# Adding the pooled attention output on the matrix engine in the first batch of an attention and gated feed-forward kernel

## The chip, the cores and the metric

The kernel runs on one core of a Trainium2 chip. The metric is the time of one execution on the device in microseconds (us), as the median of three runs. The engines are called by the names of the profile: PE is the matrix engine and PEld its weight loads, ACT is ScalarE, DVE is VectorE, POOL is GpSimd, and SP is the queue that issues most transfers.

## The reference

Shapes are 8 batches, 8 heads, 576 tokens and a head width of 64. Two attentions are added, and the sum goes through a gated feed-forward layer (512 to 1536 to 512):

```
q_d, k_d, v_d = mean over 4 neighbouring tokens of q, k, v      # 144 pooled tokens
out_up    = repeat(softmax(q_d k_d^T / 8) v_d, 4)               # each pooled row for 4 tokens
out_local = softmax(q k^T / 8 where |i - j| < 4) v              # a band of 7 tokens
x = (out_up + out_local), heads side by side                    # 4608 x 512
y = (relu(x w_gate) * (x w_val)) w_out
```

## The kernel before

The work is cut into 32 **pairs** of heads, four to a batch: pair p belongs to batch p // 4. A pair's steps carry names that the text uses with the pair's number behind them:

- `lq`, `lk`, `lv0` to `lv3`: loads of q, k and of four pieces of v, issued by SP. `cast`: q and k to 16 bits. `T`: transposes on PE; `ev0`, `ev1`, `pl`: their copies out of PSUM, `pl` being the pooled q and k.
- `Sl`, `Sd` (from pair 4 on together `S`): scores of the local and of the pooled attention. `mx`, `sub`, `exp`, `sm`, `rc`, `nrm`, `tr0`, `tr1`: the local softmax and its transposes. `dmx`, `nb` (tile `nmb`), `exd0` to `exd2` (tile `wd`), `rcd`, `nrd`: the pooled softmax. `W`, `evw` (tile `wT`): its transpose and the copy of that.
- `vc`: v to 16 bits (tile `vw`); `VP`, `vd` (tile `vdz`): v summed over four tokens on PE, and its copy.
- `V`: both products with v. The local outputs of 576 tokens lie in two PSUM banks, 288 columns in each; the pooled output of 144 columns lies behind them in the first bank. `od` (tile `od_sb`) copies the pooled output, times 0.25, to SBUF on ACT. `xa0`, `xa1` (tile `xT`) add it to the local outputs on DVE, each pooled column for four tokens.

The feed-forward layer works on chunks of tokens: `hg` and `hv` are the first products (tiles `wg_sb`, `wv_sb`; names like hg0_2 give the chunk's first token and the block of 128 of the 1536 columns), `rl` and `gm` the gate, `y` the second product (tile `wo_sb`). The first chunk needs batch 0. For columns 0 and 1 of that chunk the products are in two parts: the "a" part takes pairs 0 to 2, the "b" part pair 3.

Each step is an operation with a list of steps that it needs, one or more engines that may run it, a cost and a rank. A planner (`list_schedule`) walks through all of them once, when the program is built, and fixes the engine and the place of each. Tables of numbers by name shift the ranks (`RANKS`), delay transfers in the plan (`ASK`) and set the handicap of an engine that isn't a step's first choice (`bias`). On the chip each engine runs its steps in the planned order and waits at a step whose inputs aren't there. Where PE has nothing to do before FILL, the planner puts in products with zeros (line 1360) so that PE stays awake.

Pairs 0 to 3 are the **head** (`hd`): they run before any feed-forward work. Pairs 4 to 31 run between the products. In pairs from 8 on the transposes are transfers (`dT`, `dW`).

Of the kernel before, what the change touches and what calls it, by code (L numbers as in the profile page):

```python
# [21 lines left out]
class Op:  # L22
# [4 lines left out]
    def __init__(self, eng, dur, emit, deps=(), prio=0.0, need=None, key=None, free=(),  # L27
# [16 lines left out]
MARGIN = 0.0  # L44
# [57 lines left out]
        "lk8 cast8 ev8 pl8 mx8 exd0_8 exd1_8 nrm8 nrd8 lv0_8 lv1_8 lv3_8 vc8 VP8 V8 xa0_8 "  # L102
        "xa1_8 "
# [105 lines left out]
    ),  # L209
    -299: (  # L210
# [19 lines left out]
    ),  # L230
    -251: (
# [3 lines left out]
        "rc28 "  # L235
    ),
# [28 lines left out]
        "lk28 cast28 ev28 pl28 mx28 exp28 exd0_28 exd1_28 nrm28 nrd28 vc28 V28 xa0_28 "  # L265
        "xa1_28 "
# [10 lines left out]
    -191: (  # L277
        "pl11 "
# [95 lines left out]
    -103: (  # L374
        "pl21 "
    ),
# [14 lines left out]
        "exd0_0 exd0_3 msk16 pl27 "  # L391
# [53 lines left out]
        "T5 ev1_5 mx5 sub5 exp5 nb5 exd0_5 exd1_5 nrm5 nrd5 W5 evw5 VP5 V5 xa0_5 xa1_5 "  # L445
# [5 lines left out]
        "msk5 rc25 "  # L451
    ),
# [40 lines left out]
        "cast25 ev25 pl25 mx25 exp25 exd0_25 exd1_25 nrm25 nrd25 lv0_25 lv1_25 lv3_25 vc25 "  # L493
        "vs25 V25 xa0_25 xa1_25 "
# [4 lines left out]
    -33: (  # L499
        "lv2_26 "  # L500
    ),
    -32.5: (
        "lk26 ev26 pl26 exp26 exd0_26 exd1_26 nrm26 nrd26 lv0_26 vc26 vs26 V26 xa0_26 "
        "xa1_26 "
    ),
    -31: (
        "lk1 sub13 mx16 "
# [5 lines left out]
        "cast13 ev13 pl13 mx13 exp13 exd0_13 nrm13 nrd13 lv0_13 lv1_13 vc13 vs13 V13 xa0_13 "  # L513
# [33 lines left out]
        "dmx0 dmx1 dmx2 dmx3 vd4 dmx9 dmx11 dmx12 dmx14 dmx15 dmx16 dmx18 dmx19 dmx21 dmx22 "  # L547
        "dmx27 vc27 dmx29 dmx30 "
# [9 lines left out]
        "lv2_27 lv2_29 lv2_30 "  # L558
# [36 lines left out]
        "wg0 dmx4 sm30 "  # L595
# [9 lines left out]
    ),  # L605
    27.5: (
# [6 lines left out]
        "lk4 cast4 T4 ev0_4 ev1_4 mx4 sub4 exp4 nb4 nrm4 nrd4 W4 evw4 lv0_4 lv1_4 lv3_4 VP4 "  # L613
        "V4 xa0_4 "
# [5 lines left out]
        "y12_0 y12_1 y12_2 y14_0 y14_1 y14_2 "  # L620
    ),
# [25 lines left out]
        "cast6 T6 ev0_6 ev1_6 sub6 exp6 nb6 exd0_6 exd1_6 nrm6 nrd6 W6 evw6 lv0_6 lv1_6 "  # L647
        "lv3_6 VP6 V6 xa0_6 xa1_6 "
# [18 lines left out]
    ),  # L667
    60: (
# [9 lines left out]
        "lv0_2 "  # L678
    ),
# [56 lines left out]
    ),  # L736
    130.5: (
# [10 lines left out]
    ),  # L748
    147.5: (
        "rcd10 "  # L750
    ),
    150.5: (
        "nb31 "
# [35 lines left out]
        "cast31 ev31 pl31 mx31 exp31 exd0_31 exd1_31 nrm31 nrd31 vc31 vs31 V31 xa0_31 "  # L789
        "xa1_31 "  # L790
# [13 lines left out]
    219.5: (  # L804
        "pl23 "
    ),
    221: (
        "lv3_13 "
# [7 lines left out]
    230.5: (  # L816
        "sm25 "
    ),
# [4 lines left out]
        "sm31 "  # L823
# [11 lines left out]
        "tr0_8 sm16 pl19 exd0_19 exd1_19 "  # L835
# [61 lines left out]
    370.5: (  # L897
        "lk22 "
# [34 lines left out]
    ),  # L933
    443.5: (
# [8 lines left out]
    460.5: (  # L943
        "pl15 "
    ),
    467.5: (
        "pl6 "
# [3 lines left out]
    ),  # L951
    499: (
        "tr0_21 "
    ),
# [22 lines left out]
        "lv2_6 "  # L977
    ),
# [27 lines left out]
ASK = {"wv1": 34, "wo2": 62}  # L1006

# [63 lines left out]
def list_schedule(ops, bank_pools, eps):  # L1071
# [56 lines left out]
    while n_left:  # L1128
# [11 lines left out]
        for (i, e), s in starts.items():  # L1140
            if ends[i][1] == e and (best is None or s < best[0]):
                best = (s, e)
        assert best is not None, "the graph is stuck"
        t0, e = best
# [77 lines left out]
def kernel(  # L1222
# [10 lines left out]
    nc = tc.nc  # L1233
# [164 lines left out]
    def pair(p):  # L1398
# [325 lines left out]
        def emit_V(o):  # L1724
            for i in range(12):
                nc.tensor.matmul(  # L1726
                    out=bank[o.banks[i // 6]][:, 48 * (i % 6) : 48 * (i % 6) + 48],
                    lhsT=vw16[S3][:, i, :],
                    rhs=at2[S3][:, i, :].rearrange("p (a c) -> p a c", c=32)[:, :, 0:24],
                    start=True, stop=True)  # L1730
            n = 0
            for hh in range(2):
                for kc in range(2):
                    nc.tensor.matmul(  # L1734
                        out=bank[o.banks[0]][:, 288 : 288 + SD],
                        lhsT=vdz[S3][0:KR, hh, kc, :], rhs=wcols(hh, kc),
                        start=(n == 0), stop=(n == 3))
                    n += 1

        r["V"] = V = add(PE, 0.7 if hd else 0.56, emit_V,  # L1740
                         [*tr, vc, vdo, evw], prio=P + 40, need=(pool_, 2), key=("V", p),
                         name=f"V{p}", n=16, bias=0.0 if hd else MARGIN, late=LATE_V)
        xa = []
        t0 = b * S
        odc = add(ACT, 0.3, lambda o: nc.scalar.mul(  # L1745
            out=od_sb[S2], in_=bank[V.banks[0]][:, 288 : 288 + SD], mul=0.25),
            [V, b2.get("xa")], prio=P + 41, name=f"od{p}")
        for hf in range(2):
# [164 lines left out]
    for o in ops:  # L1913
        o.prio += SHIFT.get(o.name, 0.0)
        o.after = ASK.get(o.name, o.after)
    order = list_schedule(ops, {"F": [0, 1, 2, 3], "A": [4, 5, 6, 7]},
# [42 lines left out]
```

## Time and profile before

| | us |
|---|---|
| median of 3 runs | 364.04 (364.04 to 365.33) |
| the profiled execution | 365.24 |
| its span, first to last instruction | 363.5 |
| PE busy in the span | 352.8 (97%) |
| DVE, ACT, POOL busy | 248.4, 206.9, 201.4 |
| first feed-forward product starts | 32.60 |

The busy time of PE counts the products with zeros as well. The engines beside PE are busy for 55 to 68% of the span. The granted clock of PE is 1.00 in the whole span. What each stretch of the span is bound by is read from the stretch, not from the shares of the whole.

### The profile page before, as it was taken

Reading aid. Unit: us, or ns where it says so; the run is one execution under the profiler, and the core shown is the slowest. Engines: PE = TensorE matmul, PEld = TensorE weight load, DVE = VectorE, ACT = ScalarE, POOL = GpSimd, SP = SyncE. Lnnn points to the kernel's source line nnn. Section 1 sums busy time; section 2 is a strip of 40 time slices with the busy share of each in tenths; the row PEclk is TensorE's granted clock in tenths of the full one; section 3 lists DMA queues with packets and bytes.
Section 4 is the critical chain, followed back from the end, with each engine's and each line's share of the span. In section 5 each row is a group of like instructions: output and inputs, shape, how many; then the busy total and the mean of one; then the engine's idle time right before and its main releaser. Section 6 shows DMA issues by size and latency. Waiting matters only on the chain.

```text
span 363.5 us, 10504 instructions
## 1 busy us (share of the span) xinstructions
PE 352.8 (97%) x4241; PEld 182.2 (50%) x4241; DVE 248.4 (68%) x477; ACT 206.9 (57%) x484; POOL 201.4 (55%) x237
## 2 busy tenths in 40 slices
PE   8888999999999999999999999999989999999996
PEld 3555656445545454445444455444544454445554
DVE  4666988618987898969895986888969853322210
ACT  2477796537774757664476485768558523233222
POOL 7798574933387788683987369567785310000000
PEclk9999999999999999999999999999999999999999
DMA  7999999879999999999999999999993121011012
GB/s 189 192 276 246 192 206 301 127 181 171 272 207 214 208 276 184 271 216 253 191 220 232 172 290 165 246 239 223 200 231 81 23 85 53 0 60 59 0 70 106
DMA packets 122067, 64.80 MB, mean 178 GB/s; under 512 B 100386, under 2 KB 106402, under 8 KB 122018
## 3 DMA queue, kind: packets, MB, share of 16 engines
q1 hardware_dynamic: 116194, 59.41, 76.2%
q0 software_dynamic: 5824, 4.72, 8.6%
q8 instruction: 33, 0.54, 0.6%
q14 instruction: 16, 0.13, 0.1%
HBM read 47.59 MB, written 9.44 MB: 157 GB/s over the span
## 4 chain that ended last, share of the span: by engine, by line
PE 85%; DMA 4%; POOL 3%; SPq 2%; issue 2%; DVE 1%; ACT 1%; POOLq 0%; ACTq 0%; DVEq 0%
PE bank L1793 50%; PE bank L1859 23%; PE bank L1518 4%; DMA vw<-in_v_dram 3%; PE bank L1726 2%; PE bank L1734 2%; PE bank L1537 2%; DMA gT<-in_q_dram 1%; POOL vw L1330 1%; SPq L1675 1%; PE bank L1635 1%; PE bank L1690 1%; POOL wd L1626 1%; PE bank L1838 1%; PE bank L1456 1%
## 5 line engine op out<-in xcount | busy, mean ns | idle before, releaser
L1814 DVE TENSOR_TENSOR gT<-r,bank 128x512 f16<-128x512 f16 (+1 forms) x112 | 74.7, 667 | 65.0 <-PE bank L1793 60.6
L1793 PE MATMUL bank<-xT,wv_sb 128*128 128x512 f16 (+2 forms) x528 | 112.2, 341 | 0.9 <-ACT r L1807 0.9
L1793 PE MATMUL bank<-xT,wg_sb 128*128 128x512 f16 (+2 forms) x528 | 112.2, 341 | 0.0
L1807 ACT ACTIVATE r<-bank 128x512 f16<-128x512 f32 (+1 forms) x112 | 65.3, 584 | 65.0 <-PE bank L1793 58.1
L1859 PE MATMUL bank<-wo_sb,gT 128*128 128x512 f16 x420 | 96.6, 379 | 0.0
L1793 PEld LDWEIGHTS <-wg_sb 128*128 128x128 f16 x528 | 44.2, 98 | 46.5 <-issue 0.6
L1793 PEld LDWEIGHTS <-wv_sb 128*128 128x128 f16 x528 | 44.2, 98 | 46.0 <-issue 1.8
L1859 PEld LDWEIGHTS <-gT 128*128 128x128 f16 x420 | 39.8, 98 | 45.3 <-issue 0.4
L1868 ACT COPY y_sb<-bank 128x512 f32<-128x512 f32 x35 | 20.6, 587 | 48.7 <-PE bank L1859 48.6
L1330 POOL CAST vw<-vw 128x1536 f16<-128x1536 f32 x27 | 39.5, 1463 | 3.6 <-DMA vw<-in_v_dram 2.3
L1506 DVE TENSOR_REDUCE qkd<-qkT 128x288 f16<-128x1152 f16 x28 | 37.5, 1341 | 3.6 <-ACT qkT L1329 3.3
L1581 POOL TENSOR_TENSOR s_sb<-s_sb,mx 128x384 f32<-128x384 f32 x28 | 23.3, 833 | 27.8 <-DVE mx L1578 27.2
L1600 ACT ACTIVATE wd<-bank,nmb 128x144 f16<-128x144 f32 x96 | 35.8, 383 | 4.3 <-POOL nmb L1590 3.3
L1616 DVE STREAM_TRANSPOSE at<-e 64x384 f16<-64x384 f16 x64 | 36.4, 569 | 1.7 <-POOL e L1610 1.0
L1610 POOL TENSOR_TENSOR e<-e,rs 128x384 f16<-128x384 f16 x32 | 26.8, 841 | 16.6 <-DVE rs L1608 12.6
L1626 POOL TENSOR_TENSOR wd<-wd,rsd 128x432 f16<-128x432 f16 x32 | 29.1, 910 | 9.9 <-DVE rsd L1622 9.7
L1754 DVE TENSOR_TENSOR xT<-bank,od_sb 128x288 f16<-128x288 f32 (+2 forms) x68 | 26.8, 431 | 10.2 <-ACT od_sb L1745 10.1
L1329 ACT COPY qkT<-tq 128x1152 f16<-128x1152 f16 x23 | 27.8, 1211 | 2.9 <-DMA tq<-c 2.8
L1712 POOL TENSOR_TENSOR vs<-v 104x512 f32<-104x512 f32 x20 | 25.4, 1269 | 3.1 <-DMA v<-in_v_dram 2.8
L1587 DVE TENSOR_REDUCE nmx<-bank 128x3 f32<-128x432 f32 x32 | 19.0, 593 | 3.6 <-PE bank L1537 3.6
L1330 POOL CAST c<-qk 128x1152 f16<-128x1152 f32 x16 | 18.2, 1149 | 5.2 <-issue 2.8
L1717 POOL TENSOR_TENSOR vdz<-vs 104x256 f16<-104x256 f32 x20 | 14.6, 728 | 10.7 <-PE bank L1734 10.1
(66 smaller groups left out, 345.4 us busy)
## 6 DMA issues: line engine op xcount, KB each, us to landing
vw<-in_v_dram SPq DMA_DIRECT2D x126, 96.0 KB, 4.5
out_dram<-y_sb SPq DMA_DIRECT2D x16, 512.0 KB, 4.1
qk<-in_q_dram SPq DMA_DIRECT2D x14, 576.0 KB, 7.0
qk<-in_k_dram SPq DMA_DIRECT2D x14, 576.0 KB, 6.8
v<-in_v_dram SPq DMA_DIRECT2D x10, 640.0 KB, 7.8
wv_sb<-in_moe_w_val_dram POOLq DMA_DIRECT2D x4, 384.0 KB, 10.4
wg_sb<-in_moe_w_gate_dram POOLq DMA_DIRECT2D x4, 384.0 KB, 10.0
wo_sb<-in_moe_w_out_dram POOLq DMA_DIRECT2D x4, 384.0 KB, 8.1
```

Source lines behind the costliest of these rows:

```text
L1329: return lambda o: nc.scalar.copy(out=dst, in_=src(o))
L1330: return lambda o: engine[eng].tensor_copy(out=dst, in_=src(o))
L1506: nc.vector.tensor_reduce(out=qkd[S3].rearrange("p (x t) -> p x t", x=2), in_=qk_sums, axis=AX.X, op=ALU.add)
L1600: exd.append(add(ACT, 0.37, lambda o, i=i: nc.scalar.activation(out=_sap(wd_, 0, 128, 256 * i + K0, kd_cols), in_=_sap(dview()[:, i, :], 0 ...
L1610: r["nrm"] = nrm = add_any(either(lambda o, e: e.tensor_tensor(out=e_, in0=e_, in1=bc12(rs[S3]), op=ALU.mult), (POOL, 0.84), (DVE, 0.5)), ...
L1616: tr.append(add(DVE, 0.575, lambda o, lo=lo: nc.vector.transpose(out=at2[S3][lo : lo + 64, :, lo // 2 : lo // 2 + 32], in_=e_[lo : lo + 64 ...
L1626: r["nrd"] = nrd = add_any(either(lambda o, e: e.tensor_tensor(out=_sap(wd_, 0, 128, K0, w3), in0=_sap(wd_, 0, 128, K0, w3), in1=_sap(rsd[ ...
L1754: nc.vector.tensor_tensor(out=xT[:, kk, (c1 + lo) % XR : (c1 + lo) % XR + hi - lo].rearrange("p (t f) -> p t f", f=4), in0=bank[V.banks[hf ...
L1793: nc.tensor.matmul(out=bank[(h or o).banks[0]][:, n * x : n * x + n], lhsT=w_sb[:, kk, bass.ts(jj, 128)], rhs=xT[:, kk, x_col(t0) : x_col( ...
L1807: rl = add(ACT, 0.17 + 0.00083 * n * m, lambda o: nc.scalar.activation(out=rt[:, 0 : n * m], in_=bank[f1.banks[0]][:, 0 : n * m], func=AF. ...
L1814: gm = add(DVE, 0.15 + 0.00104 * n * m, lambda o: nc.vector.tensor_tensor(out=gT[:, js[0] : js[0] + m, pos : pos + n], in0=rt[:, 0 : n * m ...
L1859: nc.tensor.matmul(out=bank[parts[0].banks[0]], lhsT=gT[:, jj, col : col + 128], rhs=wo_sb[:, jj, :], start=(jj == 0), stop=(jj == NJJ - 1))
```

## The change

In pairs 0 to 3 the pooled output is no longer a separate product. After the twelve local products, eight more with 288 columns each add the pooled output into the same two banks; their moving operand reads each of 72 pooled columns four times. So `od` and the additions on DVE go, and `xa0`, `xa1` of these pairs become plain copies from PSUM that ACT or DVE may run. The factor 0.25 moves into the matrix that sums v, for all pairs that use it (0 to 11). Core of the diff:

```
-            sums[x, i, 12 * i + 6 * par[x] + (r[x] - 3) // 4] = 1.0
+            sums[x, i, 12 * i + 6 * par[x] + (r[x] - 3) // 4] = 0.25
...
-                    start=True, stop=True)
+                    start=not hd or i % 6 == 0, stop=not hd)
+            if hd:
+                for hf in range(2):
+                    for n in range(4):
+                        nc.tensor.matmul(
+                            out=bank[o.banks[hf]][:, 0:288], lhsT=vdz[S3][0:KR, n // 2, n % 2, :],
+                            rhs=_sap(wT[S3], 0, KR, n * SD + 72 * hf, [[1, 72], [0, 4]]),
+                            start=False, stop=(n == 3))
+                return
...
-        r["V"] = V = add(PE, 0.7 if hd else 0.56, emit_V,
+        r["V"] = V = add(PE, 1.35 if hd else 0.56, emit_V,
...
+        if not hd:
+            odc = add(ACT, 0.3, ... mul=1.0 if p < VPOOL else 0.25 ...)
+        for hf in range(2 * hd):
+            xa.append(add_any(copies(
+                xT[:, kk, x_col(t0 + 288 * hf) : x_col(t0 + 288 * hf) + 288],
+                lambda o, hf=hf: bank[V.banks[hf]][:, 0:288], (ACT, 0.41), (DVE, 0.45)),
+                [V], prio=P + 42 + hf, free=[("V", p)], name=f"xa{hf}_{p}"))
-        for hf in range(2):
+        for hf in range(0 if hd else 2):
...
-            if ends[i][1] == e and (best is None or s < best[0]):
+            if ends[i][1] == e and (best is None or (s, e != POOL) < best[:2]):
```

The last line lets POOL go first where two engines could start a step at the same planned time. The tables change as well: the shifts of 38 names in `RANKS` are other ones, a second table of shifts (`MORE`, 332 names), a second one of delays (`ASKED`) and a table of handicaps (`STAY`) are new. A line of each:

```
+    -250.0: (
+        "rc20 lv3_24 "
+    ),
...
+ASKED = {"wg2": 29.5, "wg3": 42.0, "wo1": 58.5}
...
+        "sub5 ev8 ev9 ev11 ev12 ev13 ev14 ev15 ev16 ev17 ev18 ev19 ev20 ev21 ev23 ev24 ev25 "
```

So the order changes on every engine. Three places are shown. The first is the queue of SP, from the load of pair 2's q (`gT` takes q and k of the head, `vw_64` to `vw_67` are the v buffers of pairs 0 to 3). Before:

```order
L1430 DMA gT<-in_q_dram 48x2x768
L1675 DMA vw_65<-in_v_dram 32x12x64 x3
L1675 DMA vw_64<-in_v_dram 32x12x64
L1669 DMA vw_64<-in_v_dram 29x64
L1675 DMA vw_64<-in_v_dram 32x11x64
L1675 DMA vw_64<-in_v_dram 32x12x64
L1430 DMA gT<-in_q_dram 48x2x768
L1675 DMA vw_66<-in_v_dram 32x12x64
L1430 DMA gT<-in_k_dram 48x2x768
```

The same place after the change:

```order
L1783 DMA gT<-in_q_dram 48x2x768 x2
L1783 DMA gT<-in_k_dram 48x2x768
L2028 DMA vw_64<-in_v_dram 32x12x64 x2
L2028 DMA vw_66<-in_v_dram 32x12x64
L2028 DMA vw_65<-in_v_dram 32x12x64
L2022 DMA vw_64<-in_v_dram 29x64
L2028 DMA vw_64<-in_v_dram 32x11x64
L2028 DMA vw_65<-in_v_dram 32x12x64 x2
L2028 DMA vw_66<-in_v_dram 32x12x64
```

Pair 3's q and k stand ahead of the v pieces now, and the last two pieces of pair 1's v (`vw_65`) stand behind those of pair 0.

The second place is POOL in the head (`wo_sb<-gT` are the casts of q and k, `nmb` the step nb, `e` the step nrm, `wd` the step nrd, `vw` the step vc). Before:

```order
L1330 CAST wo_sb<-gT 96x2x12x64 x3
L1380 DMA wv_sb<-in_moe_w_val_dram 128x4x384
L1380 DMA wg_sb<-in_moe_w_gate_dram 128x4x384
L1590 ISA
L1590 TENSOR_SCALAR nmb_129<-nmx_126 128x3
L1590 TENSOR_SCALAR nmb_130<-nmx_127 128x3
L1610 TENSOR_TENSOR e_92<-e_92,rs_123 128x384
L1610 TENSOR_TENSOR e_93<-e_93,rs_124 128x384
L1330 CAST vw_84<-vw_64 128x1536
L1330 CAST vw_85<-vw_65 128x1536
L1330 CAST wo_sb<-gT 96x2x12x64
L1590 TENSOR_SCALAR nmb_131<-nmx_128 128x3
```

After:

```order
L1683 CAST wo_sb<-gT 96x2x12x64 x3
L1733 DMA wv_sb<-in_moe_w_val_dram 128x4x384
L1733 DMA wg_sb<-in_moe_w_gate_dram 128x4x384
L1683 CAST wo_sb<-gT 96x2x12x64
L1943 ISA
L1943 TENSOR_SCALAR nmb_129<-nmx_126 128x3
L1963 TENSOR_TENSOR e_92<-e_92,rs_123 128x384
L1963 TENSOR_TENSOR e_93<-e_93,rs_124 128x384
L1943 TENSOR_SCALAR nmb_130<-nmx_127 128x3
L1683 CAST vw_85<-vw_65 128x1536
L1943 TENSOR_SCALAR nmb_131<-nmx_128 128x3
L1979 TENSOR_TENSOR wd_99<-wd_99,rsd_135 128x6x3x24
```

The cast of pair 3's q and k moves ahead of the first nb, and vc of pair 0 leaves POOL (it is on ACT now, as is vc of pair 2).

The third place is ACT, up to the last copies that the first feed-forward product needs (`xT` is what that product reads). Before, where the product needs what DVE adds behind the third od:

```order
L1584 ACTIVATE e_92<-s_sb_91 128x384
L1745 ACTIVATE od_sb_112<-bank_145 128x144
L1600 ACTIVATE wd_99,smd_132<-bank_144,nmb_129 128x2x3x24
L1745 ACTIVATE od_sb_113<-bank_138 128x144
L1600 ACTIVATE wd_99,smd_132<-bank_144,nmb_129 128x2x3x24 x2
L1329 CAST vdz_98<-bank_140 96x2x2x64
L1745 ACTIVATE od_sb_112<-bank_139 128x144
```

After, where the last two rows are the copies of pair 2:

```order
L1682 CAST xT<-bank_142 128x288
L1953 ACTIVATE wd_99,smd_132<-bank_143,nmb_129 128x2x3x24 x2
L1682 CAST xT<-bank_145 128x288
L1682 CAST vw_86<-vw_66 128x1536
L1682 CAST xT<-bank_138 128x288
L1682 CAST xT<-bank_141 128x288
L1682 CAST vdz_98<-bank_140 96x2x2x64
L1682 COPY wT_102<-bank_144 96x6x2x48
L1682 CAST xT<-bank_138 128x288
L1682 CAST xT<-bank_139 128x288
```

All eight copies of the head stand on ACT, and vc of pair 2 stands among them.

On PE the head now runs to V2, then VP3, the first product's first part (hg0_0a) and V3. Behind the head PE has the same steps as before in nearly the same order; towards the end some steps of pairs 28 to 31 stand earlier among the products.

More of the change, by code (lines that the diff above doesn't have):

```diff
@@ L230 @@
     ),
+    -253: (
+        "V1 "
+    ),
     -251: (
@@ L667 @@
     ),
+    59: (
+        "pl11 "
+    ),
     60: (
@@ L736 @@
     ),
+    130: (
+        "T4 "
+    ),
     130.5: (
@@ L803 @@
     ),
-    219.5: (
-        "pl23 "
+    214: (
+        "pl25 "
+    ),
+    217.5: (
+        "pl26 "
     ),
     221: (
-        "lv3_13 "
+        "pl13 lv3_13 "
     ),
@@ L951 @@
     ),
+    480.5: (
+        "sm25 "
+    ),
     499: (
         "tr0_21 "
+    ),
+    500: (
+        "pl19 "
     ),
@@ L1008 @@
+STAY = {name: by for by, names in STAY.items() for name in names.split()}
 EV = (1.2, 1.2, 0.68)
@@ L1915 @@
         o.after = ASK.get(o.name, o.after)
+        o.bias = STAY.get(o.name, o.bias)
+    for o in ops:
+        o.prio += MORE.get(o.name, 0.0)
+        o.after = ASKED.get(o.name, o.after)
+        o.bias = STAY.get(o.name, o.bias)
     order = list_schedule(ops, {"F": [0, 1, 2, 3], "A": [4, 5, 6, 7]},
```

419 lines of the change are left out of this document (370 added, 49 removed), and 5 rows, old and new, of the table MORE.

## The prediction

> **What bounds the kernel now.** I read the windows first: the busy time of each engine in stretches of the span. The columns are the stretch, its length, and the busy time with the number of instructions of PE, PEld, DVE, ACT and POOL.
>
> ```profile
> 0.00:33.00 33.00, 27.61 (x485) 15.74 (x486) 21.23 (x49) 17.11 (x50) 26.83 (x37) 1.00 1.06 229
> ...
> 41.00:100.00 59.00, 58.59 (x940) 31.77 (x938) 43.75 (x80) 39.12 (x94) 33.23 (x38) 1.00 1.02 209
> 100.00:200.00 100.00, 100.00 (x1202) 50.05 (x1194) 82.81 (x160) 62.33 (x155) 77.43 (x89) 1.00 1.08 224
> 200.00:300.00 100.00, 98.85 (x1184) 49.49 (x1183) 80.39 (x158) 61.96 (x144) 59.19 (x70) 1.00 0.89 178
> ```
>
> From 41 us to 300 us PE is busy for 257.4 of 259 us. What it does there is fixed by the reference and is the same after the change, so a microsecond lost or won ahead of 41 us reaches the end whole, and behind it there are only 1.6 us to win. The head is another matter: there PE waits for the other engines (zeros fill part of it), and its length is set by them. The chain of waits shows by which (start, length, engine and line):
>
> ```profile
> 18.17 2.73 POOL vw L1330 x2
> ...
> 30.50 0.92 POOL wd L1626
> ...
> 32.77 1.29 PE bank L1793 x6
> ...
> 42.85 0.45 PE bank L1518 x48
> ```
>
> Two vc casts on POOL, then POOL's normalising steps, and with them the first feed-forward products (the last row is for a price below). So the head now hangs on POOL. The timeline of PE shows where the products begin and what is lost before they run without holes:
>
> ```profile
> 32.60 0.81 PE L1793 MATMUL bank<-xT,wg_sb 128*128 128x512 f16 x3
> ...
> 34.33 0.68 PE L1456 MATMUL bank<-ident_sb,c 128*128 128x128 f16 x9
> 34.84 0.81 PE L1793 MATMUL bank<-xT,wg_sb 128*128 128x512 f16 x3
> ...
> 36.69 0.67 PE L1456 MATMUL bank<-ident_sb,c 128*128 128x128 f16 x9
> 38.02 0.52 PE L1518 MATMUL bank<-qkT 64*32 64x32 f16 x48 [0.67 <-DVE xT L1754]
> ...
> 40.10 1.02 PE L1793 MATMUL bank<-xT,wg_sb 128*128 128x512 f16 x4
> ```
>
> The start is 32.60. At 36.69 the transposes of pair 4 begin; such a set takes 34.84 - 34.33 = 0.51, so PE is free at 37.20 and waits 0.82 for the scores of pair 5 (a bank that DVE's additions of pair 3 hold). That is the one large hole between the start and 40.10.
>
> **The change, part by part.** *V of the head.* The price of the eight new products comes from the chain: the twelve local and the four pooled products of a V, and twelve feed-forward products with 512 columns in a row:
>
> ```profile
> 58.43 0.30 PE bank L1726 x12
> 58.73 0.25 PE bank L1734 x4
> ...
> 63.24 2.59 PE bank L1793 x12
> ```
>
> A product with 512 columns takes 2.59 / 12 = 0.216, so one with 288 takes 0.121 and eight take 0.97. Less the 0.25 of the four old ones, each V of the head grows by 0.72, from 0.55 to 1.27. No row has a moving operand that reads an element four times. The nearest is a step of two elements in the local scores of pairs from 8 on:
>
> ```profile
> 84.98 0.45 PE bank L1518 x48
> ...
> 85.64 0.33 PE bank L1690 x6
> ```
>
> With a step of one, in pair 4, the same 48 products took the same 0.45 (the row of 42.85 above). So a step costs nothing there, and I take full speed; the other bound is half speed (rival four).
>
> *What starts ACT.* POOL's queue has pair 3's cast ahead of the first nb. These rows of the timeline set its price (13.97 is used below):
>
> ```profile
> 13.97 1.57 SPq L1430 DMA_DIRECT2D gT<-in_k_dram  x1
> ...
> 15.12 0.76 POOL L1380 DMA_DIRECT2D wg_sb<-in_moe_w_gate_dram  x1
> ...
> 16.28 0.38 ACT L1600 ACTIVATE wd<-bank,nmb 128x144 f16<-128x144 f32 x1 [0.52 <-POOL nmb L1590]
> ```
>
> POOL is done with its second weight load at 15.88, and ACT's first pooled exponential follows 0.40 later; nb is 0.24 of that (a row below), so a hand-over costs some 0.08. With a cast of 1.46 in between, ACT starts at 17.74.
>
> *ACT's queue.* From there to the copies of pair 2, on which the first product waits, ACT has 29 steps in the new order. Their mean times in the head (all groups of ACT and of POOL between 11 and 33 us, name and shape, count, busy us and mean ns):
>
> ```profile
> L1600 ACT ACTIVATE wd<-bank,nmb 128x144 f16<-128x144 f32 x12 | 4.5, 390 | 1.5 <-POOL nmb L1590 1.5
> ...
> L1329 ACT COPY wT<-bank 96x576 f16<-96x576 f16 x4 | 2.6, 640 | 2.0 <-PE bank L1635 2.0
> ...
> L1584 ACT ACTIVATE e<-s_sb 128x384 f16<-128x384 f32 x4 | 2.1, 525 | 3.2 <-DVE s_sb L1571 3.2
> L1329 ACT CAST vdz<-bank 96x256 f16<-96x256 f32 x3 | 1.1, 363 | 0.2 <-PE bank L1690 0.2
> L1329 ACT CAST qkd<-bank 128x288 f16<-128x288 f32 x2 | 0.8, 423 | 0.0
> ```
>
> ```profile
> L1330 POOL CAST vw<-vw 128x1536 f16<-128x1536 f32 x4 | 5.8, 1462 | 0.0
> ...
> L1330 POOL CAST wo_sb<-gT 96x1536 f16<-96x1536 f32 x2 | 2.9, 1464 | 2.3 <-DMA gT<-in_q_dram 2.3
> ...
> L1590 POOL TENSOR_SCALAR nmb<-nmx 128x3 f32<-128x3 f32 x4 | 0.9, 242 | 1.0 <-DVE nmx L1587 0.9
> ```
>
> And a vc on ACT, from later pairs:
>
> ```profile
> L1329 ACT CAST vw<-vw x5: 1466/1474/1486, 53.0 to 269.8; 128x1536 f16<-128x1536 f32 x5
> ```
>
> Twelve exponentials at 0.39 are 4.68, two vc at 1.47 are 2.95, one pl at 0.42, two exp at 0.53 are 1.05, three vd at 0.36 are 1.09, three evw at 0.64 are 1.92, and six copies to `xT` at 0.42 (the shape of `qkd`) are 2.54: 14.65 in all. Without a wait ACT is through at 17.74 + 14.65 = 32.4. Two kinds of waits come on top. While PE runs V2 for 1.27, ACT has one evw of 0.64 to do, so it stands for 0.63. And it waits for another engine at sub2, W0, V0 and W3, for a hand-over each at least, 0.3 together. So the copies end at 33.4, and with PE's own hand-over of 0.1 the first product starts at 33.5: **0.9 later than 32.60**. POOL no longer sets the head; ACT does, since it took over two vc and the copies while it lost three od (and DVE lost the additions).
>
> *PE behind the start.* From 32.60 to 40.10 PE takes 7.50 now. The hole of 0.82 goes: V3 and the copies of pair 3 come before the transposes of pairs 4 and 5, and the copies are on ACT. VP3 (0.33, the row of 85.64 above) stands ahead of the start now, and V3 is 0.72 longer. That makes 0.82 + 0.33 - 0.72 = **0.4 won back**. What is late next there is the pl of pair 4, a step of DVE; it starts as soon as T4 is copied, and DVE no longer has additions ahead of it.
>
> *The v pieces.* In SP's queue pair 3's q and k pass the v pieces. The last piece of pair 1's v is SP's 22nd transfer now; before, the 22nd was issued at 13.97 (the row above). Where a load stands in this queue matters, since the weight loads of POOL start just then. Packets of the two queues (q0 is POOL's, q1 SP's) from 17 to 18.5 us, and from 20 to 22 us:
>
> ```profile
> q0 software_dynamic: 359, 0.28, 124.4%
> q1 hardware_dynamic: 19, 0.00, 1.4%
> ```
>
> ```profile
> q0 software_dynamic: 369, 0.28, 89.8%
> q1 hardware_dynamic: 359, 0.09, 34.0%
> ```
>
> And the time from issue to landing of a v piece issued at 13.33, and of the two issued from 15.59 on:
>
> ```profile
> DMA to landing us min/median/max: 4.4/4.4/4.4
> ...
> DMA to landing us min/median/max: 8.2/8.2/8.3
> ```
>
> I put the issue at 14.5, so the piece lands between 18.9 and 22.7; I take the middle, 20.8. POOL's vc of pair 1 waits for it, and behind it in POOL's queue stand nb2 and all nrd. ACT reaches the exponential that needs nb2 at 17.74 + 6 x 0.39 + 1.47 + 0.42 + 0.36 = 22.3, so vc must start by 22.3 - 0.24 - 1.46 - 0.16 = 20.4. **0.4 late**, and ACT's whole rest shifts by it.
>
> [...]
>
> *Behind 41 us* PE has the same steps, so I cost the moved ones at nothing. The cover is that their inputs are there when PE comes; rivals two and three say what it is worth.
>
> *The sum:* 0.9 - 0.4 + 0.4 = 0.9. The profiled execution took 365.24 (1.7 outside its span), which makes 366.1; it ran 1.2 above the median of 364.04, which makes **364.9** for the median.
>
> **The rivals.** *One: the v piece is starved to the end.* It lands at 22.7, 2.3 behind the point of 20.4 from which it decides: 364.5 + 2.3 = **366.8**, slower. For it: SP's queue got 19 packets in 1.5 us. Against it: that stretch fell behind a load of q and k, and here only two v pieces are in question.
>
> *Two: faster.* The piece is in time (364.5), and PE's waits behind the head go. These are the three that stand there now:
>
> ```profile
> 60.69 0.19 PE L1518 MATMUL bank<-qkT 64*32 64x32 f16 x2 [0.41 <-issue]
> ...
> 263.75 0.41 PE L1734 MATMUL bank<-wT,vdz 104*128 104x144 f16 x4 [0.30 <-DMA wT<-wd]
> ...
> 271.83 1.02 PE L1793 MATMUL bank<-xT,wv_sb 128*128 128x512 f16 x4 [0.85 <-ACT r L1807]
> ```
>
> Without their 1.56 it is 362.9, and without ACT's waits of 1.0 in the head 361.9; the middle is **362.4**. For it: the new order moves work from POOL to ACT and DVE in later pairs. Against it: the waits come from transfers and from ACT, not from POOL.
>
> *Three: PE waits more behind 200 us.* Scores and V of pairs 28 to 31 stand earlier among the products, and an engine that runs in order waits there. With two more waits of 0.85 and one of 0.30: 364.9 + 2.0 = **366.9**. For it: DVE is busy for 80 of 100 us there, so a step has little room to be earlier. Against it: only three waits in 259 us now.
>
> *Four: reading one element four times runs at half speed.* V2 and V3 lie on the path, 0.97 more each: 364.9 + 1.9 = **366.8**. The scores with step two speak against it.
>
> **How the numbers follow.** A measurement of this kernel can tell 0.5%, 1.8 us, from no change: faster is below 362.2, slower above 365.9. I give my forecast 0.42, and since its landing time alone spreads by 2 us, 0.10 of that is slower and 0.32 the same. Rival one has 0.18 (0.15 slower, 0.03 same), two 0.25 (0.12 faster, 0.13 same), three 0.10 (0.08 slower, 0.02 same), four 0.05 (0.04 slower, 0.01 same). That makes 0.12 faster, 0.51 the same, 0.37 slower. The range runs from rival two to just above rivals one, three and four, 362.3 to 367.0; about 2 in 10 lie outside.
>
> **What would show it.** Right: the first feed-forward product at 33.5 to 34, ACT without a gap between 17.7 and the copies of pair 2 except at V2, the hole of 0.82 gone, V of the head at 1.27. Wrong: a first exponential of ACT near 16.3; POOL idle before vc of pair 1 until 22 (rival one); products of 288 columns at 0.25 apart (four); waits of over 1 us on PE behind 41 us (three). A first product before 32.6 would break the reading that ACT bounds the new head.

## The result and the profile after

The changed kernel takes **368.89 us** (median of six runs, 366.61 to 374.82) against 364.35 for the kernel before. The run of 374.82, at a clock of 0.986, counts as slow and is left out of the ratio. That ratio is 1.0091, 95% interval 1.0063 to 1.0119, or 3.3 us slower; the two medians lie 4.5 apart. The forecast was 364.9 in a range of 362.3 to 367.0.

The profiled execution took 366.61, with a span of 364.8. It was the fastest of the six, and its granted clock is 1.000; the four others that count took 367.73 to 369.08 at a clock of 0.991 to 0.995. The windows after, with the columns of those before:

```profile
0.00:33.00 33.00, 27.92 (x486) 16.48 (x487) 21.60 (x47) 17.45 (x49) 24.47 (x35) 1.00 1.07 228
...
41.00:100.00 59.00, 59.00 (x893) 32.23 (x892) 46.15 (x85) 36.73 (x93) 34.62 (x39) 1.00 1.01 205
100.00:200.00 100.00, 98.87 (x1258) 49.76 (x1256) 83.74 (x162) 64.85 (x151) 69.88 (x81) 1.00 1.06 220
200.00:300.00 100.00, 99.33 (x1173) 49.42 (x1171) 85.03 (x160) 63.99 (x150) 58.92 (x70) 1.00 0.91 185
```

POOL has lost 2.4 us of work in the head, yet the head isn't shorter. PE's timeline tells a part of why (in brackets the idle time ahead of a row and what ended it; "issue" is a wait for nothing that the profile shows):

```profile
17.95 0.24 PE L1813 MATMUL bank<-ident_sb,wo_sb 96*128 96x96 f16 x2 [2.04 <-issue]
...
24.69 0.30 PE L1871 MATMUL bank<-qkT 64*32 64x32 f16 x20 [0.84 <-issue]
...
33.92 0.90 PE L2161 MATMUL bank<-xT,wg_sb 128*128 128x512 f16 x3
...
40.29 1.04 PE L2161 MATMUL bank<-xT,wg_sb 128*128 128x512 f16 x4
...
178.72 1.02 PE L2161 MATMUL bank<-xT,wv_sb 128*128 128x512 f16 x4 [0.35 <-ACT r L2175]
194.96 0.41 PE L2096 MATMUL bank<-wT,vdz 104*128 104x144 f16 x4 [0.77 <-DMA wT<-wd]
247.25 0.41 PE L2096 MATMUL bank<-wT,vdz 104*128 104x144 f16 x4 [0.65 <-DMA wT<-wd]
```

The first row is in the middle of one step: ten of the twelve transposes of pair 2's k ran, then PE stood for 2.04 us, and then came the last two. The view names no data that it waited for. The trail starts in the queue table of the page, and in that table for 15.0 to 16.6 us (queue, packets, MB, share of 16 engines):

```profile
q8 instruction: 33, 0.54, 0.6%
```

```profile
q8 instruction: 1, 0.02, 5.1%
```

PE's instructions come in 33 transfers of 16 KB, one for every 256 weight loads and products (2 x 4252 in all), so a block holds 128 products with their loads. In the 17 profiles of this document 24 waits of over 0.25 us behind 10 us are marked "issue". By a count of PE's products all 24 stand 94 or 95 of them behind a multiple of 128, and PE goes on 1.25 to 1.65 us after a block's landing. So such a wait is **a block of instructions that came late**. In the packets of that queue the block in question lands at 16.50, and PE goes on 1.45 later. Before, the same block landed at 15.14, and PE went on at 16.62 after a stop of 0.48. The rows of POOL and ACT behind the stop:

```profile
17.58 0.26 POOL L1943 TENSOR_SCALAR nmb<-nmx 128x3 f32<-128x3 f32 x1
...
21.06 1.46 POOL L1683 CAST vw<-vw 128x1536 f16<-128x1536 f32 x1 [1.46 <-DMA vw<-in_v_dram]
```

```profile
18.23 0.40 ACT L1682 CAST qkd<-bank 128x288 f16<-128x288 f32 x1 [1.87 <-PE bank L1813]
18.52 0.39 ACT L1953 ACTIVATE wd<-bank,nmb 128x144 f16<-128x144 f32 x1
```

The first nb is done at 17.84, but `pl2` stands ahead of the exponentials in ACT's queue and needs those two last transposes. PE's row at 24.69 is the next block end, 128 products on.

For an account I take three marks: the first feed-forward product, the first product of the second chunk (hg576_0; behind it PE has work nearly without holes), and PE's last product.

| profile of | first product | hg576_0 | last product | from hg576_0 to the last | clock |
|---|---|---|---|---|---|
| before | 32.60 | 77.48 | 360.15 | 282.67 | 1.000 |
| changed | 33.92 | 77.83 | 361.53 | 283.70 | 1.000 |
| changed, again | 35.05 | 78.96 | 363.35 | 284.39 | 0.995 |
| addition alone (`add_only`) | 33.03 | 77.82 | 359.67 | 281.85 | 0.999 |
| all moves and 119 pairs (`all_119`) | 33.15 | 77.05 | 364.93 | 287.88 | 1.000 |
| addition and 21 pairs (`add_21`) | 31.84 | 76.63 | 359.45 | 282.82 | 1.000 |

In the first profile 0.35 is lost up to hg576_0 and 1.03 behind it.

### The profile page after: what moved, and what is told of

Read it like the earlier page. It is cut to its first block, busy times and chain, and to the rows that moved or that the text cites. A ratio compares the mean times of both kernels' runs of the same rounds, so it can differ in the third digit from the quotient of the medians.

```text
span 364.8 us, 10513 instructions
## 1 busy us (share of the span) xinstructions
PE 354.9 (97%) x4252; PEld 184.0 (50%) x4252; DVE 254.3 (70%) x480; ACT 206.9 (57%) x484; POOL 194.3 (53%) x230
## 4 chain that ended last, share of the span: by engine, by line
PE 78%; DMA 11%; POOL 3%; ACT 3%; issue 2%; SPq 2%; DVE 1%; ACTq 0%; POOLq 0%
PE bank L2161 43%; PE bank L2227 22%; DMA wT<-wd 4%; DMA vw<-in_v_dram 3%; PE bank L1871 3%; DMA gT<-in_q_dram 3%; PE bank L2079 2%; PE bank L2096 2%; DMA tq<-c 1%; PE bank L1890 1%; ACT wd L1953 1%; PE bank L2043 1%; PE bank L1988 1%; PE bank L2206 1%; POOL vs L2065 1%
## 5 line engine op out<-in xcount | busy, mean ns | idle before, releaser
L1683 POOL CAST vw<-vw 128x1536 f16<-128x1536 f32 x23 | 33.6, 1463 | 5.7 <-DMA vw<-in_v_dram 2.9
L1979 POOL TENSOR_TENSOR wd<-wd,rsd 128x432 f16<-128x432 f16 x31 | 28.1, 908 | 11.1 <-DVE rsd L1975 9.2
L1934 POOL TENSOR_TENSOR s_sb<-s_sb,mx 128x384 f32<-128x384 f32 x27 | 22.4, 831 | 17.7 <-DVE mx L1931 17.4
L1963 POOL TENSOR_TENSOR e<-e,rs 128x384 f16<-128x384 f16 x29 | 24.0, 831 | 13.7 <-DVE rs L1961 10.5
L2122 DVE TENSOR_TENSOR xT<-bank,od_sb 128x288 f16<-128x288 f32 (+2 forms) x60 | 23.3, 427 | 8.3 <-ACT od_sb L2108 7.8
L1682 ACT COPY qkT<-tq 128x1152 f16<-128x1152 f16 x21 | 25.1, 1199 | 3.9 <-DMA tq<-c 3.9
L1683 POOL CAST c<-qk 128x1152 f16<-128x1152 f32 x15 | 17.1, 1147 | 15.2 <-DMA qk<-in_k_dram 8.2
L1871 PEld LDWEIGHTS <-qkT 64*32 64x32 f16 x1536 | 13.6, 90 | 12.9 <-issue 9.0
L1953 ACT ACTIVATION_READ_ACCUMULATOR wd<-bank,nmb 128x1 f32 x96 | 19.8, 206 | 0.0
```

Source lines behind the costliest of these rows:

```text
L1682: return lambda o: nc.scalar.copy(out=dst, in_=src(o))
L1683: return lambda o: engine[eng].tensor_copy(out=dst, in_=src(o))
L1871: nc.tensor.matmul(out=scv[32 * c : 32 * c + 32, i, :], lhsT=cols(hh, q0 + step * 24 * blk, 32), rhs=cols(hh, k0 + step * (24 * blk - 3), 32),
L1953: exd.append(add(ACT, 0.37, lambda o, i=i: nc.scalar.activation(out=_sap(wd_, 0, 128, 256 * i + K0, kd_cols), in_=_sap(dview()[:, i, :], 0 ...
L1979: r["nrd"] = nrd = add_any(either(lambda o, e: e.tensor_tensor(out=_sap(wd_, 0, 128, K0, w3), in0=_sap(wd_, 0, 128, K0, w3), in1=_sap(rsd[ ...
```

## The experiments

"Clock low" counts the runs whose mean clock was below 0.998.

| kernel | median us | ratio to before, 95% interval | clock low |
|---|---|---|---|
| before, beside the sets of runs below | 364.63 to 364.79 | | 5 of 68 |
| again | 368.23 | 1.0091 (1.0059 to 1.0123) | 6 of 10 |
| add_only | 365.27 | 1.0015 (0.9996 to 1.0035) | 0 of 12 |
| tables_only | 381.54 | 1.0433 (1.0398 to 1.0468) | 6 of 6 |
| vpiece | 367.54 | 1.0076 (1.0049 to 1.0104) | 4 of 10 |
| early_rcd | 368.83 | 1.0088 (1.0061 to 1.0116) | 5 of 6 |
| dw_ahead | 369.46 | 1.0112 (1.0080 to 1.0145) | 5 of 6 |
| three | 368.25 | 1.0074 (1.0047 to 1.0102) | 4 of 6 |
| zeros4 | 369.79 | 1.0122 (1.0076 to 1.0168) | 3 of 6 |
| after_119 | 368.25 | 1.0106 (1.0059 to 1.0153) | 2 of 6 |
| all_119 | 369.78 | 1.0135 (1.0095 to 1.0175) | 0 of 6 |
| before_stop | 364.50 | 0.9987 (0.9960 to 1.0015) | 5 of 12 |
| before_119 | 368.46 | 1.0102 (1.0061 to 1.0143) | 4 of 6 |
| before_75 | 369.19 | 1.0112 (1.0088 to 1.0137) | 5 of 6 |
| add_75 | 369.57 | 1.0124 (1.0098 to 1.0149) | 6 of 6 |
| add_21 | 363.41 | 0.9949 (0.9927 to 0.9971) | 1 of 10 |

**The changed kernel again.** 

> The changed kernel once more, unaltered, to see where its runs differ from its profiled execution (366.61 us at a granted clock of 1.000, while its other runs took 367.7 to 369.1 at 0.991 to 0.995). Theory (instructions and clock): PE stands for 2.04 us at 15.9 us because its next instructions land late, and with so little done there the clock of PE falls to a half for one stretch in most runs: median 368 to 369, mean clock 0.991 to 0.996, and in a profile with a clock below 1.000 the low stretch lies between 13 and 27 us, some 3.4 us long (0.005 x 367 = 1.8 us of lost clock). Rival (transfers): the runs differ by waits for transfers behind 41 us; then the low clock is a by-product, lies behind 41 us, and PE shows waits of over 1 us there.

Its profile is one at 0.995, and it shows where the clock was low (windows of 1 us; the third number from the right is the clock):

```profile
18.00:19.00 1.00, 0.47 (x4) 0.28 (x4) 0.09 (x1) 0.19 (x1) 1.00 (x3) 1.00 1.30 197
19.00:20.00 1.00, 1.00 (x15) 0.84 (x14) 0.48 (x1) 1.00 (x6) 0.85 (x2) 0.78 1.32 228
20.00:21.00 1.00, 1.00 (x15) 0.97 (x13) 0.80 (x2) 1.00 (x1) 0.00 (x0) 0.50 1.32 206
21.00:22.00 1.00, 1.00 (x63) 0.63 (x60) 0.53 (x1) 1.00 (x5) 0.00 (x0) 0.50 1.26 219
22.00:23.00 1.00, 1.00 (x14) 0.28 (x3) 0.64 (x2) 1.00 (x6) 0.66 (x1) 0.51 1.39 255
```

The loss is 0.22 + 0.50 + 0.50 + 0.49 = 1.71, so PE ran at half clock for 3.4 us. What stands ahead of that stretch, and behind 41 us, in PE's timeline, and POOL's vc of pair 1:

```profile
18.53 0.24 PE L1813 MATMUL bank<-ident_sb,wo_sb 96*128 96x96 f16 x2 [2.73 <-issue]
...
247.96 0.41 PE L2096 MATMUL bank<-wT,vdz 104*128 104x144 f16 x4 [1.75 <-DMA wT<-wd]
271.32 0.41 PE L2096 MATMUL bank<-wT,vdz 104*128 104x144 f16 x4 [1.12 <-DMA wT<-wd]
```

```profile
22.34 1.47 POOL L1683 CAST vw<-vw 128x1536 f16<-128x1536 f32 x1 [2.49 <-DMA vw<-in_v_dram]
```

The theory holds: the stop was longer, and the clock was low behind it, in the head. Of the rival, the waits behind 41 us came as well (V24 and V27 waited 2.87 for their transposed weights), but the clock wasn't low there. The v piece of pair 1 landed at 22.19 in place of 20.91. By the clock, the ten runs and the other five of the first set part into medians of 367.43 (five runs at 1.000) and 368.80 (nine at 0.995). Their ranges overlap, so the clock goes with 1.4 us and isn't all of it.

**The addition alone, and the tables alone.** The first has the addition with the tables and the tie-break of before; the second the new tables with the pooled product, `od` and the additions of before.

```
-RANKS = { ... }; MORE = { ... }; ASKED = { ... }; STAY = { ... }
+RANKS = { as before }; MORE, ASKED, STAY = {}, {}, {}
```

> The addition on PE alone, with the tables and the tie-break of before. Theory (instructions and clock): SP's queue in the head is that of before, so PE's instructions come as before (a stop of at most 0.6 us near 16 us), the clock stays at 1.000, and the time is that of before plus the longer V: 364.0 to 365.5. Rival (the addition itself costs): V2 and V3 lie on the path, two times 0.72 and the copies on ACT: 366 to 368. A faster kernel than before (under 363.5) would say that the tables cost what the addition won.

> The new tables and the tie-break with the pooled product, od and the additions of before. Theory (instructions and clock): SP's queue in the head is the new one, PE stands for about 2 us near 16 us and the clock falls below 1.000 in most runs: 367 to 369. Rival (the addition itself costs): 363.5 to 365, clock 1.000.

Near 16 us both theories hold. PE stands for 0.31 with the tables of before and for 2.14 with the new ones, whatever the pooled product (`add_only`, then `tables_only`):

```profile
16.37 1.89 PE L1363 MATMUL bank<-r 128*128 128x512 f16 x8 [0.31 <-issue]
```

```profile
17.93 0.24 PE L1813 MATMUL bank<-ident_sb,wo_sb 96*128 96x96 f16 x2 [2.14 <-issue]
```

The addition alone is level with the kernel before, although it shows a stop of its own, in the middle of V2:

```profile
32.24 0.41 PE L1738 MATMUL bank<-wT,vdz 96*128 96x288 f16 x2 [1.11 <-issue]
```

So **the tables cost what was lost, not the addition**: the changed kernel is `add_only` with the new tables (and the tie-break), and took 3.0 more in the same set of runs (368.23 against 365.27). By the marks above, its two profiles lose 0.01 and 1.14 against `add_only` up to hg576_0, and 1.85 and 2.54 behind it. The tables alone came out far worse than any theory had it. They shift ranks in a plan that was found with V's new length. My reading, which no run shows, is that the order falls apart without it; the longest waits stand in later pairs, where V isn't even changed:

```profile
198.61 0.52 PE L1871 MATMUL bank<-qkT 64*32 64x32 f16 x48 [2.88 <-ACT qkT L1682]
...
280.19 0.52 PE L1871 MATMUL bank<-qkT 64*32 64x32 f16 x48 [3.27 <-ACT qkT L1682]
```

It is no measure of the tables in their own plan. The next kernels leave the plan as it is and move single steps in the finished order.

**Single steps moved.** `vpiece`, `early_rcd`, and both with a third move (`three`):

```
+    ("lv0_2", "behind", "lv3_1"),                                   # vpiece
+    ("rcd24", "behind", "exd2_24"), ("nrd24", "ahead of", "vc25"),  # early_rcd
+    ("rcd27", "behind", "exd2_27"), ("nrd27", "ahead of", "vd29"),
+    ("pl2", "behind", "exd1_0"),                                    # three, with all above
```

> The changed kernel with one transfer of SP moved: the piece lv0_2 (pair 2's, which nobody needs before 29 us) goes behind lv3_1, the last piece of pair 1, which is then SP's 21st transfer in place of the 22nd. All else stands as it is. In two profiles of the changed kernel that piece landed at 20.91 and at 22.19, and V0 started at 26.44 and at 27.71: 1.28 and 1.27 apart. Theory (three losses: the v piece, the instruction stop with the clock, late wT behind 180 us): the piece lands by 20.8, POOL's vc of pair 1 starts by 21 in the profile, and the median falls by 0.3 to 1.0, to 367.3 to 368.0. Rival (the stop at 16 us alone sets the head): no difference, 368.2.

> The changed kernel with four steps of pairs 24 and 27 moved ahead: rcd behind the last exponential of its pair on DVE, nrd ahead of a vc (pair 24) and of a vd (pair 27) on POOL. The transfers dW24 and dW27, which V24 and V27 wait for (0.65 to 1.75 and 0 to 1.83 us in three profiles), can be issued 1 to 3 us earlier; the order on PE, ACT and SP stands as it is. Theory (late wT): no wait over 0.3 at V24 and V27 in the profile, and the median falls by 1.0 to 2.5, to 365.7 to 367.2. Rival (transfers are slow whatever their issue): the waits stay, 367.8 to 368.8.

> The changed kernel with the moves of the last two kernels of this name's set together (lv0_2 behind lv3_1; rcd and nrd of pairs 24 and 27 ahead) and one more: ACT's copy pl2 behind the first two pooled exponentials, so that ACT does not stand at it while PE's transposes of pair 2 wait for instructions (ACT started its exponentials at 18.52 and 19.10 in two profiles, while nb was there at 17.84 and 18.08). Theory (three losses): first pooled exponential at about 17.9, first feed-forward product by 33.5, no wait over 0.4 behind 41 us; median 364.5 to 366.3, 2 to 4 below the changed kernel. Rival (clock sets it): clock at 0.995 in half the runs and 366.5 to 368.

`vpiece`: POOL's vc of pair 1 waits for nothing; the median is 0.7 lower, as expected, but the intervals overlap. In its place the scores of pair 2 end last, which nb2 waits for by way of DVE (POOL's timeline):

```profile
19.15 1.45 POOL L1686 CAST vw<-vw 128x1536 f16<-128x1536 f32 x1
21.76 0.23 POOL L1946 TENSOR_SCALAR nmb<-nmx 128x3 f32<-128x3 f32 x1 [1.16 <-DVE nmx L1943]
```

`early_rcd`: V27's wait is gone, V24's isn't. SP's timeline shows why (POOL was done with nrd24 at 237.67):

```profile
239.87 0.61 SPq L1789 DMA_DIRECT2D qk<-in_k_dram  x1
240.57 1.96 SPq L2008 DMA_TRANSPOSE wT<-wd  x1
```

```profile
248.59 0.41 PE L2102 MATMUL bank<-wT,vdz 104*128 104x144 f16 x4 [2.07 <-DMA wT<-wd]
```

The transfer stood for 2.9 us in SP's queue behind the loads of later pairs. `three` has ACT's first exponential at 17.49, but also a stop of 2.01 and 6.8 us at half clock (3.42 lost from 17 to 25 us), and the scores of pair 2 came so late that nb2 stood 2.69; its first product is at 35.39. In this profile the moves in the head win nothing.

**The loads behind dW24 and dW27.**

```
+    ("lq28", "behind", "dW24"), ("lk28", "behind", "lq28"),         # with early_rcd's moves
+    ("lv0_30", "behind", "dW27"), ("lv1_30", "behind", "lv0_30"), ("lv3_30", "behind", "lv1_30"),
```

> The changed kernel with rcd and nrd of pairs 24 and 27 moved ahead, as in the kernel that moved these alone, and with SP's loads that stood ahead of the transfers dW24 (q and k of pair 28) and dW27 (three v pieces of pair 30) put behind them. In the kernel that moved rcd and nrd alone, nrd24 was done at 237.7 and dW24 still went out at 240.6, behind those loads, and V24 waited 2.07. Theory (SP's queue makes wT late): no wait over 0.4 at V24 and V27, median 366.0 to 367.4. Rival (the transfers are slow at that place whatever the order): the waits stay at 1 to 2 and the median at 368 or above.

V24's wait went; V27 still waited 1.41, and a new wait of 1.11 for ACT's `wd` came at 274.86. The theory holds for V24 alone, and the time did not fall: with one of 0.41 at 259.52, PE's waits behind 41 us still come to 2.9.

**Instruction blocks shifted.** Products with zeros at the start are cut into more and shorter ones, which moves every block's end to an earlier place in the program. `zeros4` and the 75-pair kernels cut 25 of them into four, the 21-pair kernels 7 into four, the 119-pair kernels 17 into eight.

```
+            for g in range(4):
+                c = slice(128 * g, 128 * g + 128)
+                nc.tensor.matmul(out=bank[i][:, c], lhsT=r1[0][:, 0:128], rhs=r1[0][:, c], ...
```

> The changed kernel with its first 25 products with zeros cut into four of 128 columns each, the same order otherwise: 75 more pairs of weight load and product stand ahead of the first scores, so the ends of PE's instruction blocks lie elsewhere in the head. Theory (instructions and clock): the stop of 2.04 us at 15.9 goes (the block that ends there now ends 75 pairs earlier, in the middle of the first scores, and was asked for while the zeros ran), ACT's first pooled exponential comes at about 17.7 in place of 18.5, the clock is 1.000 in most runs, and the median falls from 368.9 to 364.5 to 366.5; a shorter stop may appear at 13 us. Rival (queues): PE waited for data, not for instructions; the stop stays at 15.9 and the time at 368 to 369.

> The kernel before with its first 7 products with zeros cut into four of 128 columns each: 21 more pairs of weight load and product ahead of the first scores, the order otherwise that of before. PE's instruction block then ends 21 pairs earlier, at about 14.3 us in place of 16.1, while it is asked for at about the same time. Theory (instructions and clock): PE stops for 1.5 to 2.4 us at 14.3 us, the clock falls to a half for 3.4 us in some of the runs (mean 0.995), and the median rises by 0.7 to 2.5, to 365.4 to 367.2. Rival (PE in the head has time; POOL sets its length): 364.3 to 365.2 and a clock of 1.000.

> The kernel before with its first 17 products with zeros cut into eight of 64 columns (and 32 rows of output) each: 119 more pairs of weight load and product ahead of the first transposes, the order otherwise that of before. PE's instruction blocks of 128 pairs then end 119 pairs earlier in the program, where its own trace gives 6.4 to 7.6 us between the ends (at 11.99, 18.35, 25.95, 33.47 us), about as long as a block took to come. Theory (instructions): no stop of PE over 0.3 between 11 and 34 us other than for data, the clock at 1.000 in nearly all runs, and 363.0 to 364.2, below the kernel before (364.7). The runs of the kernel with 21 more pairs that kept the clock took 363.1 to 364.9, those at 0.995 took 364.9 to 367.6. Rival (POOL sets the head): 364.4 to 365.0.

> The changed kernel with the same 119 pairs more ahead of the first transposes. Theory (instructions and clock): the stop of 2.0 to 2.8 at 15.9 us goes, the clock is 1.000 in most runs, the first feed-forward product starts at 33.3 to 34.0, and the median falls by 0.8 to 2.0, to 366.3 to 367.5; the late wT behind 180 us stays. Rival (the v piece and POOL set the head, whatever the clock): first product at 33.9 to 35.0 and 367.8 to 368.5.

> The changed kernel with all of it together: 119 pairs more ahead of the first transposes, lv0_2 behind lv3_1 on SP, pl2 behind the first two pooled exponentials on ACT, and rcd, nrd and dW of pairs 24 and 27 ahead. Theory (three losses, each with its place): no stop at 16 us, clock 1.000 in most runs, first feed-forward product by 33.4, no wait over 0.4 at V24 and V27: 363.5 to 365.5, no slower than the kernel before (364.7). Rival (something else costs): over 366.5 although the three are gone.

`zeros4` and `after_119`: the stop at 16 goes, as the theory says, but PE then waits for POOL's cast of pair 3 (`after_119`, and 1.30 in `zeros4`):

```profile
18.30 0.68 PE L1817 MATMUL bank<-ident_sb,wo_sb 96*128 96x96 f16 x12 [1.29 <-POOL wo_sb L1683]
```

ACT's exponentials start at 18.45 and 18.58, no earlier than with the stop, and the time doesn't fall. `after_119` has the clock (four of six runs) and the first product (33.75) of its theory but the time of its rival; `zeros4` lies above the ranges of both. Under the stop there was a second bound.

`before_stop` splits by the clock. The stop came (first row), 1.45 in place of 0.48, and the clock was low behind it:

```profile
16.14 0.50 PE L1462 MATMUL bank<-ident_sb,wo_sb 96*128 96x96 f16 x8 [1.45 <-issue]
```

```profile
18.00:19.00 1.00, 1.00 (x4) 0.43 (x3) 0.99 (x3) 1.00 (x6) 1.00 (x2) 0.50 1.32 216
19.00:20.00 1.00, 1.00 (x4) 0.31 (x3) 0.95 (x3) 1.00 (x6) 1.00 (x2) 0.50 1.12 331
```

Its five runs at 0.995 have a median of 365.29, the seven at 1.000 one of 363.20: a low stretch goes with 2.1 within one kernel, of which the clock itself takes 1.7. None of the seven was profiled, so whether the stop was as long in them isn't shown.

`all_119` has every move and no stop at 16. All six runs kept the clock (0.999 or 1.000), the first product is at 33.15, and hg576_0 is at 77.05, earlier than in either kernel, although the next block end still stops PE for 0.94 at 24.0 us. So its head is no longer behind. Behind hg576_0, 4.2 more is lost than in the changed kernel's first profile (287.88 against 283.70). Eight waits of 0.3 to 0.9 there come to 4.9, against 1.8 in three; which of the moves brought them was not separated. One of them:

```profile
261.79 0.37 PE L1911 MATMUL bank<-qkd 64*32 64x144 f16 x12 [0.86 <-ACT od_sb L2129]
```

`before_119` missed: stops came up behind the head, where none were.

```profile
62.39 0.28 PE L1545 MATMUL bank<-qkd 64*32 64x144 f16 x5 [1.11 <-issue]
102.97 0.28 PE L1526 MATMUL bank<-qkT 64*32 64x32 f16 x17 [1.67 <-issue]
```

Yet the clock of that profile is low in the head, from 21.94 us on, where PE had waited for data alone (the longest for 0.81). `add_75` has the same from 21.79 us. The stretch just ahead of it in `before_119`, with PE busy for 1.74 of 3.41 us:

```profile
18.53:21.94 3.41, 1.74 (x71) 0.91 (x72) 3.30 (x9) 2.76 (x12) 3.41 (x4) 1.00 1.23 190
```

So a stop for instructions isn't the only thing that the clock fell behind.

**The addition with shifted blocks.**

> The kernel before with its first 25 products with zeros cut into four of 128 columns each, 75 pairs more ahead of the first scores. By its own trace the instruction blocks then end at 12.81, 19.27, 26.31 and 36.97 us, 6.5 to 10.7 apart, so at most one short stop near 13 is left in the head. Theory (instructions and clock): clock 1.000 in most runs, 363 to 364.5. Rival (a shift only moves the stops, also those behind the head, as 119 pairs did, which put 1.1 and 1.7 us of them at 62 and 103 us): 364.7 to 367.

> The addition on PE with the tables of before and 75 pairs more ahead of the first scores, as in the kernel before with 75 pairs. The stop of 1.11 inside V2 goes if the blocks end at 26.2 and 37.4 as its trace says. Theory (the addition is level by itself, and that stop hid a small gain): 0.3 to 1.2 below the addition alone (365.3), 364.0 to 365.0, and within 0.7 of the kernel before with the same shift. Rival (the addition costs, by V2 and V3 on the path): 1 or more above the kernel before with the same shift.

> The addition on PE with the tables of before and 21 pairs more. The kernel before with 21 pairs took 363.1 to 364.9 where the clock stayed and 364.9 to 367.6 where it fell. Theory: the same split by the clock here, about 363.5 to 365 at 1.000 and 1.5 to 2.5 more at 0.995, so that one stretch at half clock in the head costs 1.2 to 2.3. Rival (the clock follows the lateness and does not cause it): the runs at 0.995 are spread over the same range as those at 1.000.

With 75 pairs a block ends behind or among small products at 101 us. PE stood 2.49 (`before_75`) and 3.30 (`add_75`), and the clock was low with it (0.65 from 105 to 108 us in `add_75`):

```profile
103.73 1.02 PE L1799 MATMUL bank<-xT,wg_sb 128*128 128x512 f16 x4 [2.49 <-DVE at L1622]
```

```profile
104.00 0.40 PE L1546 MATMUL bank<-qkd 64*32 64x144 f16 x5 [3.30 <-issue]
```

The view credits the first wait to a step of DVE that was done 0.76 before PE went on. By its place, 94 products behind a multiple of 128, and by the landing 1.30 ahead, it is a block end like the others. So the shift moved the stops, as `before_75`'s rival says, and at a higher price than the 364.7 to 367 that it named. `add_75` is within 0.7 of `before_75`, as its theory says, but not at 364 to 365. With 21 pairs the addition alone is **0.5% below the kernel before**: 363.41, ratio 0.9949 (0.9927 to 0.9971).

```profile
15.88 0.50 PE L1465 MATMUL bank<-ident_sb,wo_sb 96*128 96x96 f16 x8 [1.31 <-issue]
...
31.84 0.81 PE L1817 MATMUL bank<-xT,wg_sb 128*128 128x512 f16 x3
```

At a full clock it is level with the kernel before at the same 21 pairs (362.86 to 364.55 against 363.06 to 364.90), so the gain goes with the shift, and nothing is won or lost by the addition. Its clock fell once in ten runs. That run took 364.45, inside the range of the others, so the price that was expected of a low stretch doesn't show here. Why the clock fell so much less often than in `before_stop`, with a stop of 1.31 against 1.45, is open.

## Why the prediction was wrong

*V of the head* was right. The eight products take 0.98 in the chain, 0.97 was forecast; rival four is out.

```profile
32.68 0.98 PE bank L2088 x8
```

*What starts ACT* was 0.8 too early: nb was there at 17.84, near the forecast start of 17.74, but ACT started at 18.52. The step took only POOL's nb as the start and left out `pl2`, which stands ahead of it and waited for PE. The first product still came at 33.92, in the span given as right (33.5 to 34), but that is luck. From its first exponential to the end of pair 2's copies ACT was busy for 13.0 us and stood for 2.9, where 14.65 of work and 1.3 of waits were forecast (the fourth number behind the length is ACT's):

```profile
18.52:34.40 15.88, 14.26 (x273) 8.91 (x272) 11.18 (x25) 13.01 (x43) 12.32 (x17) 1.00 1.22 258
```

And PE's last wait ahead of the first product is for POOL's nrd2:

```profile
31.84 0.54 PE L1988 MATMUL bank<-ident_sb,wd 128*96 128x128 f16 x6 [0.32 <-POOL wd L1979]
```

So *"POOL no longer sets the head; ACT does"* isn't borne out: ACT has gaps beyond the one at V2.

*PE behind the start* was right. The rows at 40.10 and 40.29 aren't the same place in the work: the changed kernel has done a set of transposes and one product less there. The kernel before has done the same work at this row:

```profile
39.34 0.67 PE L1456 MATMUL bank<-ident_sb,c 128*128 128x128 f16 x9
```

So 6.74 us became 6.37. That is 0.37 won back, 0.4 was forecast, and PE is 0.95 late there, 0.9 was forecast. By hg576_0 it is 0.35, in the main because the stop of 0.41 at 60.69 in the kernel before, a block end, has no counterpart there. *The v piece* landed at 20.91 (forecast 20.8) in one profile and at 22.19 in the other, inside the bounds that were given.

*"Behind 41 us ... I cost the moved ones at nothing"* failed. Behind hg576_0 1.03 was lost in one profile and 1.72 in the next. Rival three comes near with its price of 2.0, but not with its mechanism: it had PE's steps of pairs 28 to 31 stand earlier, while the waits came at V19, V24 and V27, whose inputs were later. nrd24 ended 4.1 us later than before for a V24 that stands 0.2 later, nrd27 7.6 later for a V27 6.0 later. The transfer of pair 24 went out at once (239.63, nrd24 done at 239.60); that of pair 27 stood behind v pieces in SP's queue, for 0.2 us in one profile and for about 2 in the other. The chance of 0.10 was too small. "An engine has the same steps" says nothing on whether their inputs keep their slack.

*"It ran 1.2 above the median"* failed. The profile came out at 366.61, near the forecast 366.1 by luck, since 0.35 in place of 0.9 was lost up to hg576_0 and 1.03 in place of nothing behind it. But the median lay 2.3 above the profile. Of the 4.0 between 368.89 and 364.9, 3.5 come from this step. One execution of each kernel can't carry an offset to the median (364.04 was itself 0.6 to 0.8 below the later medians of the kernel before), and a term that goes with the spread of the runs was missing: the stop for instructions, and half a clock behind it. The row that told of it stands in PE's timeline of before:

```profile
16.62 2.10 PE L1360 MATMUL bank<-r 128*128 128x512 f16 x9 [0.48 <-issue]
```

I had counted it as nothing, and the new order made 2.0 to 2.8 of it.

Why the block came later is not settled: its packet started at 15.19 in the changed kernel and at 13.80 before, while PE had done about the same work by 12 us. It goes with the tables (15.15 in `tables_only`, 13.58 in `add_only`). That the head's loads, which now stand closer in SP's queue, hold it up fits, but was not tried alone. How much of the 3.0 the stop costs is open too: no run that took it away (`zeros4`, `after_119`, `all_119`) won the time back.

## What to carry to other kernels

A wait ended by "issue" in the middle of a run of matrix products was a late block of instructions in all 24 cases here: count weight loads and products between the block ends (256 here). Moving the ends is a trial, not a cure: 21 pairs won 0.5% with the addition, 75 and 119 pairs only moved the stops. With a stop of 1.4 to 2.8 us in the head the matrix engine ran at half clock for 3.4 us (6.8 in `three` and `dw_ahead`), in some runs only, so look at the clock of every run before one profile is taken for the kernel. A table of ranks belongs to the plan that it was found with: judge it in that plan, and when it moves a step that feeds a transfer, follow the step through the transfer's queue.

## What the runs showed of the hardware

PE went on 1.4 to 1.5 us after its block had landed in the first stop of three profiles (16.50 to 17.95, 17.14 to 18.53, 15.14 to 16.62). Most block ends show no stop: the kernel before and the changed one bring 33 blocks each, and in all 17 profiles only 24 block ends behind 10 us stopped PE for over 0.25 us, by 0.3 to 3.3. In the second profile of the changed kernel PE was busy for 0.80 of the 3.50 us from 15.0 to 18.5, and the clock fell:

```profile
15.00:18.50 3.50, 0.80 (x19) 0.69 (x17) 2.50 (x7) 1.06 (x2) 3.45 (x5) 1.00 1.34 190
```

The longest stop there was 2.73 us. In the 13 falls that the profiles hold, PE had been busy for 0.4 to 1.8 of the 3.41 us just ahead (as long as the low stretch of the second profile). The first profile, busy for 1.34 of the 3.40 us from 15.3 to 18.7, kept its clock, so the busy time alone doesn't decide; what does is not shown.
